# Seven block products for eight in the first matrix product of a two-pass feed-forward kernel

## The chip, the cores and the metric

One core of a Trainium2 chip runs the whole kernel. The metric is the device time of one execution in microseconds (us), given as the median of several runs. TensorE (PE) multiplies, with its weight loads shown apart (PEld); VectorE (DVE), ScalarE (ACT) and GpSimd (POOL) do the element-wise work; SyncE's queue (SP) issues every DMA.

## What is computed

A windowed attention (8 batches, 8 heads, 512 local and 32 global rows, head size 64) gives 8 x 544 rows of 512 numbers. A feed-forward layer follows, and it is most of the work:

```python
x = np.ascontiguousarray(attn_out.transpose(0, 2, 1, 3)).reshape(B * S, H * D)   # 4352 x 512
h = x @ w_in                                                                     # 512 -> 2048
sp = np.maximum(h, 0.0) + np.log1p(np.exp(-np.abs(h)))
g = h * erf(sp)
return (g @ w_out).astype(np.float32)                                            # 2048 -> 512
```

The weights arrive as 64-bit floats and are turned into 32-bit ones on the chip.

## The kernel before

**Products.** Every operand of the feed-forward layer is split into a high and a low part (`xh`/`xl`, `winh`/`winl`, `gh`/`gl`, `wouth`/`woutl`), and a product is three matmuls: high by high, high by low, low by high. One matmul is 128x128 weights by 512 columns.

**Two passes.** The 2048 hidden columns are halved; pass one takes the first 1024 for all chunks, pass two the rest. A chunk is one batch's 512 local rows (c = 0 to 7); chunk 8 holds the 256 global rows of all batches. Per chunk `load_x` (L633) fetches x^T from the scratch `xsc` and splits it; `unit` (L666) makes 128 hidden columns of h^T, four K-blocks by three matmuls, so 12 in one PSUM bank of the pool `ps_h` (2 banks), and copies the bank to `hs`; a chunk has 8 units, 96 matmuls. `gate` (L692) runs softplus and erf on four units in one ACT block (into `sp`), multiplies by h, and splits into `gh`/`gl`. `project` (L733) makes the second product in four banks of `ps_a` (6 banks): 4 row tiles by 4 pairs of units by 6 matmuls, again 96. Chunk 8 has 4 units of 24 matmuls on 256 columns, and 48 matmuls in `project`. In pass one `project` writes its sum to the scratch `part`; in pass two it loads that into `pr` and adds it (`os<-op,pr`) before the store.

**Stages.** Pass one also holds the attention of all batches, whose steps fill the engines between the units. When the attention is done (the mark `ATTN`), `load_late` (L802) converts the weights of pass two: `load_w` (L584) loads 64-bit numbers into `raw` (3 buffers), builds the 32-bit number in `top_...` with four DVE operations, and splits it. Five of the eight late units are converted in pass one, the rest at the start of pass two.

**Order.** `Program.schedule` (L129) writes out the order of each engine's instructions by a list schedule: every step has a key (its due time, some 5.4 us each), a planned duration for each engine that may run it, and inputs and outputs; at each planned moment an engine takes the ready step with the lowest key. A result that another engine hands to PE counts as ready 0.8 later (`SLACK`). The engines then run in that fixed order and wait for each other on semaphores. Chunk c of pass ps starts at key s = 4(17 ps + 2c); its units lie at s to s+7, its projection from s+8.29 on in steps of 2.

Of the kernel before, what the change touches and what calls it, by code (L numbers as in the profile page):

```python
# [20 lines left out]
P = 128  # L21
WB = 32
# [3 lines left out]

SINCE, COLD, FILL, TICK, HEAT = 0.75, 3.5, 50.0, 3.41, 3200
# [6 lines left out]
WB0, WBS = 50.7, 3.09  # L34
# [206 lines left out]
def kernel(  # L241
# [342 lines left out]
    def load_w(key, src, name, HI, LO, i, deps):  # L584
        RAW = mbuf([P, 512], I64, f"raw_{name}", "raw", 3)
        load(key - RLEAD, RAW, src, 524, deps, also=[HI, LO])
        TOP = mbuf([P, 512], I32, f"top_{name}", ("wt", "wr")[i % 2], 1)
# [4 lines left out]
        add({"ACT": 0.7}, key, lambda: act(HI.ap[:, i, :], word(1).bitcast(F32), AF.Abs), [RAW], [HI])  # L592

        def bits():
            dve.tensor_scalar(
                TOP.ap, word(1), 3, 0x3FFFFFF8, op0=ALU.logical_shift_left, op1=ALU.bitwise_and
            )
            dve.scalar_tensor_tensor(
                TOP.ap, word(1), s32(0xC0000000), TOP.ap, op0=ALU.bitwise_and, op1=ALU.bitwise_or
            )  # L600
            dve.scalar_tensor_tensor(
                TOP.ap, word(0), 29, TOP.ap, op0=ALU.logical_shift_right, op1=ALU.bitwise_or
            )

        def normal():
            a = TOP.ap.bitcast(F32)
            dve.scalar_tensor_tensor(
                a, HI.ap[:, i, :].bitcast(F32), NORMAL, a, op0=ALU.is_gt, op1=ALU.mult
            )

        add({"DVE": 1.55}, key, bits, [RAW], [TOP])
        add({"DVE": 0.6}, key, normal, [HI], [TOP])
        add({"ACT": 0.62, "DVE": 0.35}, key, lambda e: copy(e, HI.ap[:, i, :], TOP.ap.bitcast(F32)), [TOP], [HI])
        add(
            {"POOL": 1.27, "DVE": 0.6},
            key,
            lambda e: vec[e].tensor_tensor(
                LO.ap[:, i, :], TOP.ap.bitcast(F32), HI.ap[:, i, :].bitcast(F32), ALU.subtract
            ),
            [HI, TOP],  # L620
            [LO],
        )

# [9 lines left out]
    def load_x(ps, c, key):  # L633
# [3 lines left out]
        for i in range(2):  # L637
            RAW = mbuf([P, 2 * SL], F32, f"rx_{ps}_{c}_{i}", "raw", 3)
# [27 lines left out]
    def unit(ps, c, v, X, key):  # L666
# [21 lines left out]
        SPb = mbuf([P, SL], F32, f"sp_{nm}", "sp", 7)  # L688
        add({"ACT": 0.58, "DVE": 0.69}, key, lambda e: copy(e, Hb.ap, HP.ap.rearrange("p a t -> p (a t)")), [HP], [Hb])
        return Hb, SPb  # L690

    def gate(ps, c, us, key, first):  # L692
        def erf():
            table(SET_SOFTPLUS)
            for Hb, SPb in us:
                act(SPb.ap, Hb.ap, AF.Softplus)
            table(SET_ERF)
            for _, SPb in us:
                act(SPb.ap, SPb.ap, AF.Erf)
            if ps == 0:  # L700
                table(SET_EXP)
# [5 lines left out]
            [TAB, *(x[0] for x in us)],  # L707
            [x[1] for x in us],
        )
        G = []  # L710
        for v, (Hb, SPb) in enumerate(us, first):
            nm = f"{ps}_{c}_{v}"
            k = key + 0.01 * v
            GH = mbuf([P, SL], F32R, f"gh_{nm}", "gh", 5)
            GL = mbuf([P, SL], F32R, f"gl_{nm}", "gl", 5)
            add({"DVE": 0.75, "POOL": 1.5}, k, lambda e, SPb=SPb, Hb=Hb: vec[e].tensor_tensor(SPb.ap, SPb.ap, Hb.ap, ALU.mult), [Hb], [SPb])
            add({"DVE": 0.43, "ACT": 0.62}, k, lambda e, SPb=SPb, GH=GH: copy(e, GH.ap, SPb.ap), [SPb], [GH])
            add({"DVE": 0.75, "POOL": 1.5},
                k,
                lambda e, SPb=SPb, GH=GH, GL=GL: vec[e].tensor_tensor(GL.ap, SPb.ap, GH.ap.bitcast(F32), ALU.subtract),  # L720
# [3 lines left out]
            G.append((GH, GL))  # L724
# [8 lines left out]
    def project(ps, c, G, key):  # L733
# [3 lines left out]
        def mm2(t, u):  # L737
            WH, WL = W["out", ps, u]
            for a in range(2):
                GH, GL = G[2 * u + a] if c < B else G[u]  # L740
                s0 = P * t + (0 if c < B else 256 * a)
                lh, ll = (g.ap[:, s0 : s0 + P] for g in (GH, GL))
                first = u == 0 and a == 0
                last = u == NU - 1 and a == 1
                pe(OP[t].ap, lh, WH.ap[:, a, :], start=first, stop=False)
                pe(OP[t].ap, lh, WL.ap[:, a, :], start=False, stop=False)
                pe(OP[t].ap, ll, WH.ap[:, a, :], start=False, stop=last)

        for t in range(nt):
            if c == B:  # L750
                at = lambda u: key + u + 0.01 * t
            else:
                at = lambda u: key + 2 * u + 0.01 * t
            for u in range(NU):
                Gs = [x for g in (G[2 * u : 2 * u + 2] if c < B else G[u : u + 1]) for x in g]
                add({"PE": 1.37}, at(u), lambda t=t, u=u: mm2(t, u), [*Gs, *W["out", ps, u]], [OP[t]], heat=3072)
            k = at(NU - 1)
            O = mbuf([P, DM], F32, f"os_{ps}_{c}_{t}", "os", 2)
# [43 lines left out]
    def load_late(i):  # L802
        kind, src, u = ("in", w_in, i) if i < NU else ("out", w_out, i - NU)
        load_unit(kind, src, 1, u, late[2 * i], late[2 * i + 1], WB0 + WBS * i, [ATTN])

    late = [(wb_pool, f"b{i}") for i in range(11)] + [
        (wpool, t) for t in ("ih0", "il0", "ih1", "il1", "ih2")
    ]
    for i in range(2 * NU):
        if i < 5:  # L810
            load_late(i)
    for ps in range(2):
        for c in range(NCHT):
            s = NU * (17 * ps + 2 * c)
            n = NV if c < B else NU
            if ps == 1 and c == 0:
                for i in range(5, 2 * NU):
                    load_late(i)
            X = load_x(ps, c, s - XLEAD)
            us = [unit(ps, c, v, X, s + v) for v in range(n)]  # L820
            last = ps == 1 and c == NCHT - 1
            G = []
            for a, z in ((0, 2), (2, 3), (3, 4)) if last else [(i, i + 4) for i in range(0, n, 4)]:
                G += gate(ps, c, us[a:z], s + z + GOFF, a)
            project(ps, c, G, s + 4 + POFF)
# [76 lines left out]
```

## Time and profile before

| | us |
|---|---|
| median of 3 runs | 976.32 (976.29 to 978.1) |
| span of the profiled execution | 971.6 |
| PE busy | 937.7 (97%) |
| DVE, ACT, POOL busy | 553.7, 537.8, 308.3 |
| DMA | 127.6 MB, 41.9% of 16 engines |

```profile
PE   8977998999999999999999999999999999999996
DVE  5888999682665674855965399233424342333332
PEclk9988999999999999999999999999999999999998
DMA  9788956481475644823431233113314040311203
```

Each digit is one fortieth of the span (24.3 us) in tenths. Attention and pass one's projections fill the left half; pass two begins near 577 us, in the 24th digit.

### The profile page before, as it was taken

What the parts mean: (1) busy time and instruction counts of PE and PEld (TensorE: products, weight loads), DVE (VectorE), ACT (ScalarE), POOL (GpSimd) and SP (SyncE); (2) the same over time, 40 slices, a digit from 0 to 9 for tenths busy, and PEclk for the clock granted to TensorE, in tenths of its full rate; (3) what the DMA queues carried; (4) which work ended last, traced back from release to release, by engine and by line L of the source; (5) the groups of instructions that cost most, each with busy time, mean ns of one, the idle gap of its engine ahead of it and who ended that gap; (6) DMA issues with size and microseconds to landing.
All of it is one profiled execution on the core that took longest, in us unless ns stands there. A gap on an engine that the chain in (4) does not pass through costs nothing.

```text
span 971.6 us, 22208 instructions
## 1 busy us (share of the span) xinstructions
PE 937.7 (97%) x9068; PEld 757.9 (78%) x9068; DVE 553.7 (57%) x1386; ACT 537.8 (55%) x876; POOL 308.3 (32%) x230
## 2 busy tenths in 40 slices
PE   8977998999999999999999999999999999999996
PEld 6756766778777777778888888888888888888895
DVE  5888999682665674855965399233424342333332
ACT  4354685454646445736777656545655454555670
POOL 2242473322242232322533246312214221212140
PEclk9988999999999999999999999999999999999998
DMA  9788956481475644823431233113314040311203
GB/s 348 229 267 265 316 148 213 125 280 28 143 223 152 183 147 133 253 68 100 152 108 44 91 129 128 65 32 98 86 45 131 1 131 0 109 46 42 87 1 108
DMA packets 79741, 127.63 MB, mean 131 GB/s; under 512 B 12184, under 2 KB 37784, under 8 KB 79640
## 3 DMA queue, kind: packets, MB, share of 16 engines
q1 hardware_dynamic: 79640, 126.22, 41.9%
q8 instruction: 71, 1.16, 0.5%
q14 instruction: 30, 0.25, 0.1%
HBM read 99.45 MB, written 26.74 MB: 130 GB/s over the span
## 4 chain that ended last, share of the span: by engine, by line
PE 87%; DVE 6%; DMA 4%; issue 1%; ACT 1%; SPq 0%; DVEq 0%; ACTq 0%
PE op L279 38%; PE h L279 35%; PE o L279 3%; PE s L279 3%; PE t L280 2%; PE spare L279 2%; DVE top_out L291 2%; PE ga L279 1%; DMA rx<-xsc 1%; PE go L279 1%; DMA xsc<-xT 1%; PE gt L280 1%; DVE top_in L291 1%; DVE sm L291 1%; DMA part<-os 1%
## 5 line engine op out<-in xcount | busy, mean ns | idle before, releaser
L279 PE MATMUL h<-xh,winh 128*128 128x512 f32 (+1 forms) x576 | 221.1, 384 | 0.0
L279 PE MATMUL h<-xh,winl 128*128 128x512 f32 (+1 forms) x576 | 217.8, 378 | 0.0
L279 PE MATMUL h<-xl,winh 128*128 128x512 f32 (+1 forms) x576 | 217.6, 378 | 0.0
L279 PE MATMUL op<-wouth,gh 128*128 128x512 f32 x544 | 217.1, 399 | 0.2 <-DVE pt L291 0.2
L279 PE MATMUL op<-wouth,gl 128*128 128x512 f32 x544 | 212.2, 390 | 0.0
L279 PE MATMUL op<-woutl,gh 128*128 128x512 f32 x544 | 212.1, 390 | 0.0
L291 POOL TENSOR_TENSOR sp<-sp,hs 128x512 f32<-128x512 f32 x73 | 105.6, 1468 | 220.8 <-ACT sp L281 220.8
L291 DVE TENSOR_TENSOR gl<-sp,gh 128x512 fp32r<-128x512 f32 x77 | 70.4, 918 | 109.1 <-ACT gh L281 108.7
L281 ACT ACTIVATE gh<-sp 128x512 fp32r<-128x512 f32 x124 | 74.7, 627 | 98.9 <-PE op L279 76.6
L281 ACT ACTIVATE hs<-h 128x512 f32<-128x512 f32 x82 | 48.9, 597 | 137.6 <-PE h L279 137.4
L279 PEld LDWEIGHTS h<-xh,winh 128*128 128x128 f32 x576 | 108.4, 188 | 21.1 <-issue 0.8
L279 PEld LDWEIGHTS h<-xh,winl 128*128 128x128 f32 x576 | 108.4, 188 | 20.4
L279 PEld LDWEIGHTS h<-xl,winh 128*128 128x128 f32 x576 | 108.6, 188 | 19.4
L291 POOL TENSOR_TENSOR gl<-sp,gh 128x512 fp32r<-128x512 f32 x59 | 86.1, 1464 | 112.9 <-ACT gh L281 90.6
L279 PEld LDWEIGHTS op<-wouth,gh 128*128 128x128 f32 x544 | 102.2, 188 | 22.7 <-issue 1.0
L279 PEld LDWEIGHTS op<-wouth,gl 128*128 128x128 f32 x544 | 102.2, 188 | 21.9
L279 PEld LDWEIGHTS op<-woutl,gh 128*128 128x128 f32 x544 | 102.3, 188 | 19.3
L282 ACT ACT_TABLE_LOAD x90 | 115.5, 1283 | 2.3 <-PEq L889 0.7
L291 DVE COPY hs<-h 128x512 f32<-128x512 f32 x54 | 37.1, 686 | 110.8 <-PE h L279 110.6
L291 POOL TENSOR_TENSOR xl<-rx,xh 128x512 fp32r<-128x512 f32 (+1 forms) x40 | 52.3, 1328 | 119.4 <-ACT xh L281 72.8
L291 POOL TENSOR_TENSOR sm<-sm,mx 128x512 f32<-128x512 f32 x34 | 38.3, 1130 | 139.4 <-DVE mx L291 95.9
L291 DVE TENSOR_TENSOR sp<-sp,hs 128x512 f32<-128x512 f32 x63 | 61.0, 986 | 31.6 <-ACT sp L281 31.5
(75 smaller groups left out, 1212.4 us busy)
## 6 DMA issues: line engine op xcount, KB each, us to landing
vb<-in_vB_dram SPq DMA_DIRECT2D x64, 325.0 KB, 3.6
rx<-xsc SPq DMA_DIRECT2D x32, 512.0 KB, 4.8
va<-in_vA_dram SPq DMA_DIRECT2D x64, 195.0 KB, 3.9
k<-in_kE_dram SPq DMA_DIRECT2D x32, 384.0 KB, 5.6
q<-in_qT_dram SPq DMA_DIRECT2D x32, 272.0 KB, 4.6
part<-os SPq DMA_DIRECT2D x34, 256.0 KB, 3.0
pr<-part SPq DMA_DIRECT2D x34, 256.0 KB, 3.5
out_dram<-os SPq DMA_DIRECT2D x34, 256.0 KB, 3.7
```

Source lines behind the costliest of these rows:

```text
L279: pe = lambda n, *a, **k: pinned(nc.tensor.matmul(n, *a, **k))
L280: tr = lambda *a, **k: pinned(nc.tensor.transpose(*a, **k))
L281: act = lambda *a, **k: pinned(nc.scalar.activation(*a, **k))
L282: table = lambda name: pinned(nc.scalar.preload_act_table_set(name))
L291: return lambda *a, **k: pinned(f(*a, **k))
```

## The change

Pass two's local rows are taken by pairs of batches (chunks 2pr and 2pr+1). The pair's first product is a 2x2 by 2x2 block product: the weight blocks are hidden columns v and v+4 (rows of blocks) by the two halves of K, the other factor is the two halves of K by the two batches. Strassen's scheme in Winograd's form makes it with seven block products in place of eight. One **quad** q (of 4) stands for units q and q+4 of both batches: seven products of 6 matmuls, 42 where four units had 48.

- **Weights** (`convert_in`). Seven forms (three blocks as they are, four sums) are built after `ATTN` at keys 46.5 and 54.5, split, and written to the scratch `wq`, two tiles of 896 KB a quad. `quad_weights` loads both before each quad (two buffers each); the first two quads of pair 0 use the tiles as they were built. The four units of `w_out` are converted at keys 71 to 74.
- **The pair's other factor** (`pair_blocks`). Four 512 KB loads, four sums, seven blocks split into high and low. Each block has one buffer.
- **Products.** Banks a and c lie in `ps_h`, b and d in `ps_a`. Banks a, c and d are used twice: the first product is read out (`move` or `fold`), then a second is added on top in the same bank and read out again. Two moves (ACT or DVE) and five folds (DVE: bank plus an SBUF tile) replace four copies.
- **Keys.** Quad q of a pair lies at s+4q, s = 68+16pr; its gates at s+11, +17, +20, +25; its two projections from s+15 and s+23 on. `project` takes its units in the order 0, 2, 1, 3, loads the partial sum straight into `os` (4 buffers, before 2) and adds in place.
- **Global rows** of pass two stay last; they use four of the seven weight forms and the same number of matmuls. In pass one they come before the last batch.
- `raw` has 5 buffers in place of 3, and a scratch area for DMA descriptors is cut to 1024 bytes.

The diff, cut to its core:

```diff
+RAWS = 5
...
-WB0, WBS = 50.7, 3.09
+CV0, CVS, CVO = (46.5, 54.5), 1.8, (71.0, 72.0, 73.0, 74.0)
+QLEAD2, XDEL = 4.0, 1.6
+GATE1, GATE2, PROJ1, PROJ2 = (11.0, 17.0), (20.0, 25.0), 15.0, 23.0
+LAST = (0, 2, 1)
...
+class Part:
+    def __init__(self, whole, n):
+        self.whole, self.n, self.pool = whole, n, None
+        self.writers, self.readers = [], []
+    @property
+    def ap(self):
+        return self.whole.ap[:, self.n]
...
-        RAW = mbuf([P, 512], I64, f"raw_{name}", "raw", 3)
+        RAW = mbuf([P, 512], I64, f"raw_{name}", "raw", RAWS)
...
-    def project(ps, c, G, key):
+    def project(ps, c, G, at, order, after=None):
...
+            for n, rows in enumerate(order):
+                need = [x for g, _, v in rows for x in (*G[g], *W["out", ps, v // 2])]
+                add(
+                    {"PE": 0.685 * len(rows)},
+                    at(n) + 0.01 * t,
+                    lambda t=t, n=n: mm2(t, n),
+                    list(dict.fromkeys(need)) + ([PART[after, t]] if after is not None and n == 0 else []),
+                    [OP[t]],
+                    heat=1536 * len(rows),
+                )
+            k = at(len(order) - 1) + 0.01 * t
+            O = mbuf([P, DM], F32, f"os_{ps}_{c}_{t}", "os", 4)
...
-                PR = mbuf([P, DM], F32, f"pr_{c}_{t}", ("wt", "wr")[t % 2], 1)
-                load(k - NU + 2, PR, part[c][P * t : P * t + P, :], 262, [PART[c, t], W["out", 1, NU - 1][1]])
+                load(k - NU + 2, O, part[c][P * t : P * t + P, :], 262, [PART[c, t]])
...
-                    lambda t=t, O=O, PR=PR: dve.tensor_tensor(O.ap, OP[t].ap, PR.ap, ALU.add),
-                    [OP[t], PR],
-                    [O],
+                    lambda t=t, O=O: dve.tensor_tensor(O.ap, OP[t].ap, O.ap, ALU.add),
+                    [OP[t]],
+                    [O, PART[c, t]],
...
+    NQ = NU
+    A11, A12, A22, S1, S2, S3, S4 = range(7)
+    wq = [[dram.tile([P, 7, 2, P], F32, name=f"wq{q}_{x}") for x in range(2)] for q in range(NQ)]
+    WQ = {(q, x): fixed(None) for q in range(NQ) for x in range(2)}
...
+    def convert_in(u, key):
+        top = lambda n: View(Buf(wb_pool, [P, 512], F32, f"c{n}_{u}", f"x{n}", 1))
+        T = {}
+        for n, (v, i) in enumerate(((u, 0), (u + 2, 0), (u + 2, 1), (u, 1))):
+            T[v - u, i] = top(n)
+            ABS = View(Buf(wb_pool, [P, 512], F32, f"ca_{u}_{n}", "x5", 1))
+            to_fp32(key + CVS * n, w_in[1, v, i], f"l_in_{v}_{i}", T[v - u, i], ABS, [ATTN])
...
+        a11, a12, a21, a22 = T[0, 0], T[0, 1], T[2, 0], T[2, 1]
+        part_of(A11, a11, key)
+        k = key + 2 * CVS
+        part_of(A22, a22, k)
+        sum_of(s1, a21, a22, ALU.add, k)
+        sum_of(a21, a11, a21, ALU.subtract, k)
+        part_of(S1, s1, k + 0.3)
+        part_of(S3, a21, k + 0.6)
+        sum_of(a11, s1, a11, ALU.subtract, k + 0.9)
+        part_of(S2, a11, k + 1.2)
+        k = key + 3 * CVS
+        part_of(A12, a12, k)
+        sum_of(a12, a12, a11, ALU.subtract, k + 0.3)
+        part_of(S4, a12, k + 0.6)
...
+                    lambda x=x, t=t, q=2 * u + r: dma(wq[q][x], t.ap.bitcast(F32)),
+                    [t],
+                    [WQ[2 * u + r, x]],
+                    moved=918.0,
...
+    def quad_weights(name, q, key):
+        HL = [Buf(wb_pool, [P, 7, 2, P], F32R, f"wq{x}_{name}", f"q{x}", 2) for x in range(2)]
+        for x, t in enumerate(HL):
+            add(
+                {"SP": 0.06},
+                key,
+                lambda x=x, t=t: dma(t.ap.bitcast(F32), wq[q][x]),
+                [WQ[q, x]],
+                [t],
+                moved=918.0,
+            )
+        return HL
...
+        k = key + 0.2
+        block("B11", 0, R[0, 0], k)
+        sum_of(T, R[0, 1], R[0, 0], ALU.subtract, k)
+        sum_of(R[0, 1], R[1, 1], R[0, 1], ALU.subtract, k + 0.1)
+        block("T1", 3, T, k + 0.1)
+        sum_of(T, R[1, 1], T, ALU.subtract, k + 0.1)
+        block("T2", 1, T, k + 0.1)
+        block("B21", 2, R[1, 0], k + 0.2)
+        block("B22", 4, R[1, 1], k + 0.3)
+        block("T3", 5, R[0, 1], k + 0.4)
+        sum_of(R[1, 0], R[1, 0], T, ALU.subtract, k + 0.4)
+        block("T4", 6, R[1, 0], k + 0.5)
+        return blocks
...
+    def products(name, q, X, key, held=None):
+        QH, QL = held or quad_weights(name, q, key - QLEAD2)
+        bank = {
+            n: Buf(pool, [P, SL], F32, f"p{n}_{name}", tag, m)
+            for n, (pool, tag, m) in zip("abcd", ((ps_h, "h", 2), (ps_a, "a", 6)) * 2)
+        }
+        def mm(n, m, x, start):
+            o, (HI, LO) = bank[n].ap, X[x]
+            for j in range(2):
+                wh, wl = (t.ap[:, m, j, :] for t in (QH, QL))
+                xh, xl = HI.ap[:, j, :], LO.ap[:, j, :]
+                more = dict(skip_group_check=True)
+                pe(o, wh, xh, start=start and j == 0, stop=False, **more)
+                pe(o, wh, xl, start=False, stop=False, **more)
+                pe(o, wl, xh, start=False, stop=j == 1, **more)
+        def product(n, m, x, start, k):
+            add({"PE": 1.37}, k, lambda: mm(n, m, x, start), [QH, QL, *X[x]], [bank[n]], heat=3072)
...
+        PAIR = mbuf([P, 2, SL], F32R, f"pair_{name}", ("xh", "xl")[q % 2], 3)
+        V, Z = Part(PAIR, 0), Part(PAIR, 1)
+        f32 = lambda b: b.ap.bitcast(F32) if b in (V, Z) else b.ap
...
+        k = [key + 4 * i / 7 for i in range(7)]
+        product("a", A11, "B11", True, k[0])
+        move(U, "a", k[0])
+        product("b", S2, "T2", True, k[1])
+        fold(U, U, "b", k[1])
+        product("a", A12, "B21", False, k[2])
+        move(C, "a", k[2])
+        product("c", S1, "T1", True, k[3])
+        fold(V, U, "c", k[3], [PAIR])
+        product("d", S3, "T3", True, k[4])
+        fold(V, V, "d", k[4])
+        product("c", S4, "B22", False, k[5])
+        fold(Z, U, "c", k[5])
+        product("d", A22, "T4", False, k[6])
+        fold(U, U, "d", k[6])
+        return (C, U), (Z, V), PAIR
...
+            for i, (m, x) in enumerate((((A11, "B1"), (A12, "B2")), ((S1, "B1"), (A22, "D")))[r]):
...
+    s = -NV
+    for c in [*range(B - 1), B, B - 1]:
+        s += NU if c == B - 1 else NV
+        n = NV if c < B else NU
+        X = load_x(0, c, s - XLEAD)
+        us = [unit(0, c, v, X, s + v) for v in range(n)]
+        G = {}
+        for a in range(0, n, 4):
+            G |= gate(0, c, us[a : a + 4], s + a + 4 + GOFF)
+        key = s + 4 + POFF
+        if c < B:
+            project(0, c, G, lambda n: key + 2 * n, [[(2 * u + a, 0, 2 * u + a) for a in range(2)] for u in range(NU)])
+        else:
+            project(0, c, G, lambda n: key + n, [[(u, 256 * a, 2 * u + a) for a in range(2)] for u in range(NU)])
+    for u in range(2):
+        first = convert_in(1 - u, CV0[u])
+    for n, u in enumerate((0, 2, 1, 3)):
+        load_unit("out", w_out, 1, u, (wpool, f"oh{u}"), (wpool, f"ol{u}"), CVO[n], [ATTN])
+    s0 = 17 * NU
+    turns, ACTS = (), fixed(None)
+    AFTER = {0: first[0], 1: [W["out", 1, u][1] for u in LAST]}
+    for pr in range(B // 2):
+        s = s0 + 4 * NU * pr
+        X = pair_blocks(pr, s - XDEL)
+        one, two = [], []
+        for q in range(NQ):
+            a, b, more = products(f"{pr}_{q}", q, X, s + 4 * q, first.get(q) if pr == 0 else None)
+            one += [(q, a[0], ()), (q + 4, a[1], ())]
+            two += [(q, b[0], (more,)), (q + 4, b[1], (more,))]
+        order = [[(v, 0, v) for v in (2 * u, 2 * u + 1)] for u in (0, 2, 1, 3)]
+        for us, c, g, at in ((one, 2 * pr, GATE1, PROJ1), (two, 2 * pr + 1, GATE2, PROJ2)):
+            G = {}
+            for h in range(2):
+                turn = fixed(None)
+                G |= gate(1, c, us[4 * h : 4 * h + 4], s + g[h], turns, [turn], [ACTS])
+                turns = [turn]
+            project(1, c, G, lambda n: s + at + 2 * n, order, c - 1 if c else None)
+    s = s0 + 4 * NU * (B // 2)
+    X = last_blocks(s - XLEAD)
+    us = [last_unit(q, X, s + q) for q in range(NQ)]
+    G = {}
+    for a, z in ((0, 2), (2, 3), (3, 4)):
+        G |= gate(1, B, us[a:z], s + z + GOFF)
+    key = s + 4 + POFF
+    project(1, B, G, lambda n: key + n, [[(q, 0, q), (q, 256, q + 4)] for q in range(NQ)])
...
-    nc = _bacc.Bacc("TRN2", target_bir_lowering=False, num_devices=1)
+    nc = _bacc.Bacc("TRN2", target_bir_lowering=False, num_devices=1, dynamic_dma_scratch_size=1024)
```

## Rows read from the trace of the kernel before

**Rows 1.** The page: span and busy time of each engine.
```profile
span 971.6 us, 22208 instructions
PE 937.7 (97%) x9068; PEld 757.9 (78%) x9068; DVE 553.7 (57%) x1386; ACT 537.8 (55%) x876; POOL 308.3 (32%) x230
```
**Rows 2.** Windows: from:to, length, busy (instructions), granted clock, DMA share, GB/s; seven of pass two, summed.
```profile
600.00:650.00 50.00, 50.00 (x222) 41.44 (x221) 18.39 (x24) 25.39 (x40) 17.19 (x12) 1.00 0.16 53
...
sum 350.00, PE 350.00 PEld 291.86 DVE 126.05 ACT 185.24 POOL 95.49; mean PE 50.00 PEld 41.69 DVE 18.01 ACT 26.46 POOL 13.64
```
**Rows 3.** Windows of pass one's start, and of the end.
```profile
0.00:50.00 50.00, 43.88 (x959) 34.70 (x959) 34.31 (x134) 19.81 (x38) 12.55 (x15) 0.97 0.84 282
50.00:100.00 50.00, 40.76 (x818) 30.61 (x815) 41.97 (x163) 25.56 (x58) 17.54 (x16) 0.86 0.88 278
...
950.00:971.60 21.60, 12.41 (x55) 9.95 (x53) 3.41 (x5) 0.63 (x1) 0.00 (x0) 0.88 0.35 117
```
**Rows 4.** Chain that ended last, around pass two's first `h`: start, us, what.
```profile
512.17 5.44 PE h L279 x24
517.62 5.44 PE op L279 x24
...
576.82 8.16 PE h L279 x36
```
**Rows 5.** Windows around the start of pass two.
```profile
560.00:580.00 20.00, 20.00 (x107) 17.28 (x106) 19.19 (x25) 11.72 (x17) 7.95 (x5) 1.00 0.34 105
580.00:600.00 20.00, 20.00 (x90) 16.54 (x89) 19.69 (x20) 15.64 (x26) 14.75 (x10) 1.00 0.39 134
```
**Rows 6.** Tiles of pass two, 600 to 950 us: durations in ns, min/median/max.
```profile
L291 DVE TENSOR_TENSOR os<-op,pr x30: 676/691/693, 650.3 to 948.9; 128x512 f32<-128x512 f32 x30
L281 ACT ACTIVATE hs<-h x39: 575/598/604, 606.1 to 942.0; 128x512 f32<-128x512 f32 x39
L291 DVE TENSOR_TENSOR gl<-sp,gh x45: 678/693/1595, 605.7 to 938.6; 128x512 fp32r<-128x512 f32 x45
L291 DVE CAST xh<-rx x14: 285/418/1003, 609.5 to 876.1; 128x512 fp32r<-128x512 f32 x12, 128x256 fp32r<-128x256 f32 x2
L291 DVE TENSOR_TENSOR xl<-rx,xh x16: 414/677/1236, 610.2 to 919.8; 128x512 fp32r<-128x512 f32 x14, 128x256 fp32r<-128x256 f32 x2
L291 POOL TENSOR_TENSOR xl<-rx,xh x14: 1191/1294/1303, 612.0 to 877.5; 128x512 fp32r<-128x512 f32 x12, 128x256 fp32r<-128x256 f32 x2
```
**Rows 7.** DVE timeline, one conversion of half a late unit: start, us.
```profile
569.37 0.43 DVE L291 TENSOR_SCALAR top_out<-raw_out 128x512 int32<-128x512 int32 x1
569.83 1.42 DVE L291 SCALAR_TENSOR_TENSOR top_out<-raw_out,top_out 128x512 int32<-128x512 int32 x2
571.35 0.69 DVE L291 SCALAR_TENSOR_TENSOR top_out<-wouth,top_out 128x512 f32<-128x512 f32 x1
```
**Rows 8.** DMA issues of 600 to 950 us: KB each, median us to landing.
```profile
pr<-part SPq DMA_DIRECT2D x32, 256.0 KB, 3.5
out_dram<-os SPq DMA_DIRECT2D x29, 256.0 KB, 3.8
rx<-xsc SPq DMA_DIRECT2D x11, 512.0 KB, 4.8
```
**Rows 9.** Timeline of the end: start, us, what.
```profile
962.02 0.39 PE L279 MATMUL op<-wouth,gl 128*128 128x512 f32 x1
962.45 0.69 DVE L291 TENSOR_TENSOR os<-op,pr 128x512 f32<-128x512 f32 x1 [0.67 <-PE op L279]
```
**Rows 10.** Chain that ended last, a hand-over from ACT to PE.
```profile
65.33 0.94 ACT xn L281 x4
66.27 0.04 issue
66.32 1.12 PE t L280 x4
```
**Rows 11.** Waits of PE over the span, the longest: us, times, longest.
```profile
PE t L280 <- ACT xn L281: 3.5, 2, 2.6
```

More of the change, by code (lines that the diff above doesn't have):

```diff
@@ L582, in mbuf, with to_fp32 @@
         return Buf(mp, shape, dtype, name, tag, bufs)
[L584 to L587 removed]
+    def to_fp32(key, src, name, TOP, ABS, deps):
+        RAW = mbuf([P, 512], I64, f"raw_{name}", "raw", RAWS)
+        load(key - RLEAD, RAW, src, 524, deps, also=[TOP.buf, ABS.buf])
         def word(n):
@@ L605, in normal @@
-        def normal():
[L606 to L613, printed above, removed]
+            top = TOP.ap().bitcast(I32)
+            dve.tensor_scalar(top, word(1), 3, 0x3FFFFFF8, op0=ALU.logical_shift_left, op1=ALU.bitwise_and)
@@ new lines, in bits @@
+            dve.scalar_tensor_tensor(
+                top, word(1), s32(0xC0000000), top, op0=ALU.bitwise_and, op1=ALU.bitwise_or
+            )
+            dve.scalar_tensor_tensor(top, word(0), 29, top, op0=ALU.logical_shift_right, op1=ALU.bitwise_or)
+        def normal():
+            a = TOP.ap()
+            dve.scalar_tensor_tensor(a, ABS.ap().bitcast(F32), NORMAL, a, op0=ALU.is_gt, op1=ALU.mult)
+        add({"DVE": 1.55}, key, bits, [RAW], [TOP.buf])
+        add({"DVE": 0.6}, key, normal, [ABS.buf], [TOP.buf])
@@ L614, in load_w, with split @@
+    def split(key, TOP, HI, LO):
+        add({"ACT": 0.62, "DVE": 0.35}, key, lambda e: copy(e, HI.ap(), TOP.ap()), [TOP.buf], [HI.buf])
         add(
@@ L723, in gate @@
             )
-            G.append((GH, GL))
+            G[v] = (GH, GL)
         return G
@@ new lines, in mm2 @@
+        def mm2(t, n):
+            for m, (g, c0, v) in enumerate(order[n]):
+                WH, WL = W["out", ps, v // 2]
+                s0 = P * t + c0
+                lh, ll = (x.ap[:, s0 : s0 + P] for x in G[g])
+                first = n == 0 and m == 0
+                last = n == len(order) - 1 and m == len(order[n]) - 1
+                pe(OP[t].ap, lh, WH.ap[:, v % 2, :], start=first, stop=False)
+                pe(OP[t].ap, lh, WL.ap[:, v % 2, :], start=False, stop=False)
+                pe(OP[t].ap, ll, WH.ap[:, v % 2, :], start=False, stop=last)
@@ L801 @@
     add({"SP": 0.01}, HKEYS[-1][1] + 0.5, lambda: None, [], [ATTN])
[L802 to L825, printed above, removed]
+    NQ = NU
@@ new lines, in last_blocks, with block @@
+    def last_blocks(key):
+        n = B * SG
+        blocks, R = {}, []
+        for i in range(2):
+            R.append(mbuf([P, 2, n], F32, f"rg_{i}", "raw", RAWS))
+            R[i].view = None
+            load(key + 0.1 * i, R[i], xsg[2 * P * i : 2 * P * i + 2 * P, :].rearrange("(k p) t -> p k t", p=P), 525, XSG)
+        def block(name, m, A, k):
+            HI, LO = (Buf(pool, [P, 2, n], F32R, f"g{x}_{name}", tag) for x, (pool, tag) in zip("hl", XTAG[2 * m : 2 * m + 2]))
+            add({"DVE": 0.5, "ACT": 0.62}, k, lambda e: copy(e, HI.ap, A.ap), [A], [HI])
+            add(
+                {"POOL": 1.3, "DVE": 0.7},
+                k,
+                lambda e: vec[e].tensor_tensor(LO.ap, A.ap, HI.ap.bitcast(F32), ALU.subtract),
+                [A, HI],
+                [LO],
+            )
+            blocks[name] = (HI, LO)
+        block("B1", 0, R[0], key + 0.2)
+        block("B2", 1, R[1], key + 0.3)
+        add({"DVE": 0.7}, key + 0.3, lambda: dve.tensor_tensor(R[1].ap, R[1].ap, R[0].ap, ALU.subtract), [R[0]], [R[1]])
+        block("D", 2, R[1], key + 0.4)
+        return blocks
```

183 lines of the change are left out of this document (134 added, 49 removed).

## The prediction

> **What bounds the kernel now.** I read the page's busy times first: PE works 937.7 of 971.6 us, no other engine more than 57% [rows 1]. [...] The chain that ended last says the same: it runs from one run of matmuls to the next, 24 of them in 5.44 us, in `h` and in `op` alike [rows 4]. That is 0.2267 us a matmul. The waits of PE, the longest of them 3.5 us in all [rows 11], are all in attention steps. [...]
>
> **What is removed.** A pair of batches has 2 x 96 = 192 first-product matmuls before and 4 quads x 7 products x 6 = 168 after. Four pairs save 4 x 24 = 96 matmuls of the full 512 columns, 96 x 0.2267 = **21.8 us** [rows 4]. The second product and the global rows keep their count. In pass two PE has no idle time to hide this in, so it all lies on the path [rows 2]. [...]
>
> **Element-wise work in the loop.** Per pair: 16 copies of h go (0.60 us on ACT, 0.69 on DVE) [rows 6]; 8 moves come (4.8 us) and 20 folds. A fold reads one bank and one SBUF tile as `os<-op,pr` does, 0.69 us, so 13.8 us on DVE. Blocks are 14 half-tiles instead of 8: six more casts (0.42 to 0.60 each) and six more low parts (0.68 on DVE, 1.29 on POOL), 7 to 11 us. Four sums of 1024 columns are twice the 0.68 or 1.29 each, 5 to 10 us. Against 10 us removed that is some +25 us a pair, over three engines. Before, a pair's time (2 x 192 x 0.2267 = 87 us) holds (126 + 185 + 95)/350 x 87 = 101 us of such work [rows 2]; after, about 126 in three times 81.6 us. DVE goes from 36% to some 58%. No engine becomes the bound of the loop, so this costs nothing as throughput, and the cover is PE's own work. What it can cost is latency, next.
>
> **The reused banks.** In a quad three products (the third, sixth and seventh) go into a bank that must be read first: 16 quads x 3 = 48 new waits of PE on ACT or DVE. The same wait, `h` on a read of its bank, exists before, but with a second bank free. Between the first use and the reuse lies at least one other product, 6 x 0.2267 = 1.36 us. Needed are the hand-over from PE (the last matmul starts at 962.02 and lasts 0.39, the DVE step starts at 962.45, so 0.04) [rows 9], the read, 0.69 [rows 6], and the hand-over back, 0.05 by the step from ACT to PE [rows 10]: 0.78 us, which leaves 0.58. A longer operation may sit ahead in DVE's queue: `gl<-sp,gh` has a median of 0.69 but a maximum of 1.60 us [rows 6]. With one such ahead the wait is up to 1.0 us; with a group of the second product (1.36 us) also between, there is none. The planner counts a result for PE as ready 0.8 late, so it places such a group whenever one is ready, and from the second quarter of a pair on one nearly always is (keys s+7 to s+13 and s+15 to s+21 overlap the quads). Bounds for the loop: 0 and 48 x 1.0 = 48 us. I take **+1.5**, near the lower end, since the nearest wait of that kind, on `h` banks, is zero in 350 us [rows 2].
>
> **The streamed weights.** 18 quad loads of 1.8 MB, 33 MB in 386 us (576.8 to 962.4 [rows 4, 9]), add some 86 GB/s to the 53 of the first window of pass two [rows 2]. That is well under the 282 GB/s that the first 50 us moved [rows 3]. One quad's two tiles take between 1.8 MB / 282 GB/s = 6.5 us and, by 512 KB in 4.8 us [rows 8], twice 8.4 us; I take 8. A load may start when the quad two before it is done; the quad between lasts 9.5 us alone and some 20 with its share of projections. In the loop that is hidden. SP issues in order, so behind a load that waits for its buffers stand the partial sums and the stores; the partial sums (3.5 us) are asked for two keys, some 10 us, ahead [rows 8]. Nothing in the loop.
>
> **The start of pass two.** This is where I put the largest loss. DVE is busy 19.2 and 19.7 of 20 us there already [rows 5], and PE is not held up, because its queue is deep. After the change the conversions of `w_in` come earlier, where there is room, but all four units of `w_out` are converted here: 8 halves at 0.43 + 1.42 + 0.69 = 2.5 us on DVE [rows 7], 20 us, and casts and low parts besides. Add pair 0's blocks (14 casts, 14 low parts, 4 sums: 21 to 37 us over the three engines), 14 us of folds and the last batch's gate. In the meantime PE has pass one's last projection (96 matmuls, 21.8 us) and the four quads (38.1 us), and no projection of pass two before key 83, so for some two quads there is no filler: 6 waits of 0 to 1.0 us, and a wait of quad 3 for its weights of 0 to 7 us (16.8 against 9.5). Between 0 and 13 us; I take **+3**, since the same saturation costs nothing before.
>
> **Pass one and the end.** Two more `raw` buffers let two 512 KB weight loads, 1.0 MB or 3.7 us at 282 GB/s, go out ahead of attention's loads where DMA is the limit [rows 3]. That can delay attention by up to 3.7 us, or bring later weights and x in earlier by as much: -4 to +4, I take **+1**. The global chunk moved ahead of the last batch brings the same matmuls; nothing. At the end the same four-tile projection, now of batch 7, ends last instead of two tiles: the chain after the last matmul, DVE 0.69 and a store of 3.8 us [rows 8, 9], stays. Six partial sums share four `os` buffers there, so one may load only after a store: 0 to 3 us, I take **+0.5**.
>
> **Sum.** -21.8 + 1.5 + 3 + 1 + 0.5 = -15.8 us. The span goes from 971.6 to 955.8. The median lies 4.7 us above the profiled span (976.3 - 971.6), so 960.5.
>
> **The rivals.**
> - *The start of pass two runs dry.* DVE's backlog there (for it: 39 of 40 us busy [rows 5]; against it: no wait of PE in the same stretch) costs its full 13 us and the waits of the loop a few more: 6 us more than I took to 15 more, 967 to 976.
> - *All hidden, and pass one gains.* No new wait, and the earlier weight loads bring the -4: 976.3 - 21.8 - 4 = 950.5. For it: PE waits for nothing after attention [rows 2]. Against it: the first stage is full of DMA, and bytes do not shrink [rows 3].
> - *Slower: the reused bank.* At its place, the third, sixth and seventh product of a quad, PE stands until DVE has worked off two operations. Two at 1.0 us over the cover of 0.58, plus the fold, is a wait of about 1.0 us; at 48 places 48 us, at half of them 24, which gives 976.3 - 15.8 + 24 = 984.5. It decides from 21.8/48 = 0.45 us a wait, less 0.1 for the other losses. Against it: the room of 1.36 us that each filler gives, and DVE at 58%. [...]
> - *No change.* The order written out places the quads' work so that the saved matmuls reappear as idle time of the same length, at any mixture of the places above: 976 within 2.
>
> **How the numbers follow.** My forecast, 952.5 to 967, gets 0.58; the dry start 0.17, of which 0.02 within the band of no change; all hidden 0.10; slower 0.12, of which 0.02 within the band; no change 0.03. The range 950.5 to 974 holds the forecast, 0.14 of the dry start and 0.08 of the all-hidden case, together 0.80. A difference of 0.2% (2 us) is about what a measurement of this kernel can tell from none. Faster by more: 0.58 + 0.10 + 0.15 = 0.83. Within: 0.02 + 0.02 + 0.03 = 0.07. Slower: 0.10.
>
> **What would show it.** In the profile of the changed kernel pass two should have 672 product matmuls of 512 columns besides the global rows, 0.227 us apart, with windows of PE at 50.00 of 50 between the second pair and the last. Waits of PE on DVE or ACT steps that write `u`, `c` or `pair` are the reused banks: under 2 us in all if I am right, over 20 if the slower case holds. Waits on `wq` DMAs would be the streamed weights. The first 60 us of pass two should hold what loss there is, and DVE should be near full in them. Pass one's end (the last `h` of its units) within 4 us of before confirms that term. I would be wrong most likely through DVE's plan: its steps are planned at 0.72 or 0.75 us, and where POOL runs beside it they last up to 1.6 [rows 6].

## The result and the profile after

The changed kernel takes **966.35 us** (median of 4 runs, 964.19 to 969.97) against 976.88 us: ratio **0.9902**, 95% interval 0.9874 to 0.9929. That is 10.5 us less, where 15.8 were forecast; it lies within the range. A second set of runs beside the experiments gave 0.9909 (0.9878 to 0.9940). The profiled execution spans 962.2 us, 9.4 less than before [rows 1].

The page's busy times, and three of its rows of 40 slices:

```profile
span 962.2 us, 22283 instructions
PE 920.8 (96%) x8962; PEld 740.6 (77%) x8962; DVE 645.2 (67%) x1488; ACT 536.1 (56%) x886; POOL 394.1 (41%) x289
...
PE   8988989989999999999999999979999999999996
...
DVE  5799888954476575754777799799556446544462
...
PEclk9999999999999999999999999998999999999998
```

PE is busy 16.9 us less, not 21.8, and idle 41.4 us instead of 33.9 [rows 1]. The 7 in PE's row is the 27th slice, 626 to 650 us: the start of pass two, with DVE at 7 to 9 tenths around it. The windows say where (from:to, length, busy of PE, PEld, DVE, ACT, POOL with instructions, granted clock, DMA share, GB/s):

```profile
620.00:630.00 10.00, 6.12 (x26) 4.76 (x25) 8.82 (x11) 4.35 (x9) 6.41 (x5) 0.98 1.01 398
630.00:640.00 10.00, 10.00 (x39) 8.06 (x38) 8.91 (x14) 3.31 (x7) 2.26 (x2) 0.85 0.43 149
640.00:650.00 10.00, 7.30 (x33) 5.71 (x31) 10.00 (x8) 7.49 (x12) 8.77 (x6) 1.00 0.45 177
650.00:660.00 10.00, 8.88 (x27) 7.07 (x28) 10.00 (x9) 4.04 (x8) 9.36 (x7) 0.66 0.00 0
...
560.00:720.00 160.00, 151.32 (x644) 123.23 (x643) 125.92 (x150) 83.60 (x132) 82.71 (x52) 0.97 0.49 178
720.00:900.00 180.00, 180.00 (x810) 149.63 (x809) 94.70 (x124) 96.71 (x148) 86.06 (x60) 1.00 0.46 162
```

From 720 to 900 us, where the last two pairs of batches run, PE is busy 180.00 of 180 at a granted clock of 1.00, as in [rows 2]. Between 560 and 720 it lacks 8.7 us of busy time. With each of the two long stands the granted clock falls (0.85 and 0.66 in the windows of 10 us): the next 8 and 13 matmuls run at 0.50 (the windows of these matmuls stand in the last section). Waits of PE over 560 to 720 us (us in total, times, longest), and the one kind after it:

```profile
PE pc L295 <- DVE pair L307: 4.0, 2, 3.9
PE pa L295 <- DVE u L307: 3.8, 1, 3.8
PE pd L295 <- DVE pair L307: 0.8, 1, 0.8
...
PE h_g L295 <- DMA wq_g<-wq: 1.7, 2, 1.5
```

The first three are the reused banks: a product that must wait for a fold or a move. They add up to 8.6 us, where the prediction named under 2 us as the sign that it was right and over 20 as that of the slower rival. The timeline shows what DVE did instead (start, us, what; its idle time before in brackets):

```profile
617.66 1.57 DVE L307 TENSOR_SCALAR top_out<-raw_out 128x512 int32<-128x512 int32 x1
619.26 1.42 DVE L307 SCALAR_TENSOR_TENSOR top_out<-raw_out,top_out 128x512 int32<-128x512 int32 x2
620.60 0.42 DVE L307 TENSOR_SCALAR top_out<-raw_out 128x512 int32<-128x512 int32 x1
621.05 2.48 DVE L307 SCALAR_TENSOR_TENSOR top_out<-raw_out,top_out 128x512 int32<-128x512 int32 x2
...
628.31 0.69 DVE L307 TENSOR_TENSOR pair<-u,pc 128x512 f32<-128x512 f32 x1
629.05 0.50 PE L295 MATMUL pc<-xh_B,wq 128*128 128x512 f32 x1 [3.88 <-DVE pair L307]
...
641.85 5.82 DVE L307 CAST xh_B<-rx 128x512 fp32r<-128x512 f32 x4
647.59 2.88 DVE L307 CAST xh_T<-rt 128x512 fp32r<-128x512 f32 x2
650.39 0.68 DVE L307 COPY u<-pa 128x512 f32<-128x512 f32 x1
651.12 0.79 PE L295 MATMUL pa<-xh_B,wq 128*128 128x512 f32 x1 [3.83 <-DVE u L307]
```

Two things stand ahead of the fold in DVE's queue: conversions of `w_out`, and then the next pair's casts, six in 8.6 us (641.85 to 650.47), 1.44 us each on average while POOL works beside them, where the median before is 0.42 [rows 6].

**An account by stage.** I counted in the traces how many matmuls of the two products are still to start at a given moment, each start once and a 256-column one as half. A stretch of length L in which the number falls by N has lost L - N x 0.2267 us (0.2267 us a matmul, as in [rows 4]). A 256-column matmul takes 0.12 us, a little over the half, so the global rows show some 0.6 us that nobody lost.

| | left at 450 | left at 560 | left at 720 | lost 560 to 720 | left at 900 | last starts |
|---|---|---|---|---|---|---|
| before | 2253 | 1770 | 1065 | 0.2 | 271 | 962.0 |
| changed | 2141 | 1659 | 1017 | **14.5** | 224.5 | 953.5 |

With 96 matmuls less, 1674 would be left at 560; the 15 below that are 3.4 us gained in pass one. Then 14.3 us are lost to the start of pass two, 0.3 from 720 to 900, and 2.1 from there to the end of the last matmul (3.0 against 1.0; 1.7 of it are the waits on `wq_g`, at a granted clock of 1.00 from 900 to 950 us), while what follows the last matmul is 0.9 shorter. -21.8 - 3.4 + 14.3 + 0.3 + 2.1 - 0.9 = -9.4, the difference of the spans.

### The profile page after: what moved, and what is told of

Its sections match the earlier page's. It is cut to its first block, busy times and chain, and to the rows that moved or that the text cites. A ratio compares the mean times of both kernels' runs of the same rounds, so it can differ in the third digit from the quotient of the medians.

```text
span 962.2 us, 22283 instructions
## 1 busy us (share of the span) xinstructions
PE 920.8 (96%) x8962; PEld 740.6 (77%) x8962; DVE 645.2 (67%) x1488; ACT 536.1 (56%) x886; POOL 394.1 (41%) x289
## 4 chain that ended last, share of the span: by engine, by line
PE 81%; DVE 10%; DMA 5%; issue 2%; ACT 1%; SPq 1%; POOL 0%; DVEq 0%; ACTq 0%; POOLq 0%
PE op L295 35%; PE h L295 16%; PE pd L295 4%; PE pc L295 4%; PE pa L295 4%; PE o L295 3%; PE s L295 3%; PE t L296 2%; DVE top_out L307 2%; PE pb L295 2%; PE spare L295 2%; PE ga L295 1%; DMA raw_out<-in_w_out_dram 1%; DMA vb<-in_vB_dram 1%; DVE xl_T L307 1%
## 5 line engine op out<-in xcount | busy, mean ns | idle before, releaser
L295 PE MATMUL h<-xh,winh 128*128 128x512 f32 (+1 forms) x288 | 112.3, 390 | 0.0
L295 PE MATMUL h<-xh,winl 128*128 128x512 f32 (+1 forms) x288 | 109.0, 378 | 0.0
L295 PE MATMUL h<-xl,winh 128*128 128x512 f32 (+1 forms) x288 | 108.9, 378 | 0.0
L307 POOL TENSOR_TENSOR sp<-sp,hs 128x512 f32<-128x512 f32 x40 | 59.8, 1515 | 51.5 <-ACT sp L297 51.5
L297 ACT ACTIVATE sp<-sp 128x512 f32<-128x512 f32 x136 | 74.9, 620 | 0.4
L307 DVE CUSTOM_DVE_ANT_0 sm<-s,cs 128x128 f32<-128x128 f32 x256 | 57.8, 284 | 21.7 <-PE s L295 18.4
L297 ACT ACTIVATE sm<-sm 128x512 f32<-128x512 f32 x64 | 39.9, 630 | 44.0 <-POOL sm L307 31.6
L295 PEld LDWEIGHTS h<-xh,winl 128*128 128x128 f32 x288 | 54.2, 188 | 10.5
L295 PEld LDWEIGHTS h<-xh,winh 128*128 128x128 f32 x288 | 54.3, 188 | 10.3 <-issue 0.8
L295 PEld LDWEIGHTS h<-xl,winh 128*128 128x128 f32 x288 | 54.3, 189 | 9.1
```

What stands on the lines that cost most here:

```text
L295: pe = lambda n, *a, **k: pinned(nc.tensor.matmul(n, *a, **k))
L297: act = lambda *a, **k: pinned(nc.scalar.activation(*a, **k))
L307: return lambda *a, **k: pinned(f(*a, **k))
```

## The experiments

Three theories for these 14 us, which the expectations below call 13. **DVE queue**: at the start of pass two DVE has too much work, and the folds stand behind it. **Stream**: weights or x arrive late. **Bank**: returning to a bank costs by itself. The last has the trace against it already (nothing lost in 180 us of the loop). Ratios are to runs of the kernel before on the same chip; the changed kernel's are 0.9902 and 0.9909. The counts come from one profiled execution of each run. It is the fastest of four of the changed kernel, the slowest of four in e1, v0 and v1, the fastest of ten in e3 and in e5 order, so counts and ratios need not add up.

| run | ratio (95%) | left at 450, 560, 720 | lost 560 to 720 |
|---|---|---|---|
| changed, again | 0.9909 (0.9878 to 0.9940) | 2142, 1660, 1018 | 14.5 |
| e1 less conversion | 0.9790 (0.9736 to 0.9845) | 2154, 1672, 1004 | 8.6 |
| e2 casts on ACT | 0.9844 (0.9805 to 0.9883) | 2146, 1664, 996 | 8.6 |
| e3 keys spread | 0.9935 (0.9910 to 0.9960) | 2121, 1639, 1016 | 18.8 |
| e4 both | 0.9906 (0.9877 to 0.9935) | 2128, 1646, 1001 | 13.8 |
| e5 raw 3 | 1.0102 (1.0071 to 1.0133) | 2129, 1647, 1091 | 34.0 |
| e5 order | 1.0036 (1.0009 to 1.0064) | 2123, 1640.5, 1061 | 28.6 |
| e6 double stream | 0.9997 (0.9966 to 1.0027) | 2139, 1657, 1025 | 16.7 |
| v0 early | 0.9770 (0.9747 to 0.9793) | 2137, 1655, 957 | 1.8 |
| v2 early, 4 forms | 0.9749 (0.9720 to 0.9778) | 2148, 1666, 968 | 1.8 |
| v1 early, 4 forms, ACT | 0.9773 (0.9730 to 0.9815) | 2160, 1678, 982 | 2.2 |
| v3 as v2, old order | **0.9704** (0.9661 to 0.9747) | 2140, 1657, 952 | 0.2 |

**The changed kernel again.**

> The changed kernel as it is, once more beside the others, for a comparison on the same chip. All theories: 0.990 of before, within 0.003, with some 13 us lost between 560 and 720 us.

It gave 965.35 us and the same stands.

**Less conversion work, same order of instructions.**

```diff
         def bits():
...
             dve.tensor_scalar(top, word(1), 3, 0x3FFFFFF8, op0=ALU.logical_shift_left, op1=ALU.bitwise_and)
+            if name.startswith("out_1"):
+                return
...
         def normal():
+            if name.startswith("out_1"):
+                return
```

> Same order of instructions as the changed kernel, but the late conversion of w_out does only the first of its four DVE operations (the number's other bits are left out, so the output is not the reference's); 8 x (1.42 + 0.69) = 17 us of DVE work leave the start of pass two. Theory 'DVE queue': the folds come earlier, the stand of 3.9 us behind top_out goes with its slow-clock tail, the one behind the casts shrinks; 5 to 9 us below the changed kernel's 966.4, so 957 to 961. Rival 'stream' (weights and x arrive late in the full DMA of 620 to 630 us): 966 within 2. Rival 'bank' (the return to the same bank costs by itself): 966 within 2.

956.24 us, a little better than the best expected. The waits of PE between 560 and 720 us:

```profile
PE pa L295 <- DVE u L307: 3.3, 1, 3.3
PE pc L295 <- DVE pair L307: 1.6, 2, 1.4
```

The stand behind `top_out` fell from 4.0 to 1.6 us and the other stayed, 3.3. Every DMA and every matmul stands where it stood in the order, so neither stream nor bank can explain it. 5.9 us of the 14.5 came back. The profiled execution (960.08) spans 4.1 us less than the changed kernel's: its pass one is 13 matmuls, 2.9 us, behind, and 0.8 more are lost from 720 to 900; 1.5 less after that and 0.4 less behind the last matmul make up the sum. Where the further gain of the median lies is not shown.

**Casts on ACT.**

```diff
-            add({"DVE": 1.2, "ACT": 1.22}, k, hi, [A], [HI])
+            add({"ACT": 1.22}, k, lambda: hi("ACT"), [A], [HI])
```

> The high parts of the pair blocks are cast on ACT only (planned 1.22), so the DVE casts that last 1.44 us a half beside POOL go. Theory 'DVE queue': the stand of 3.8 us behind xh_B and xh_T goes, the other stays: 3 to 6 us below the changed kernel, 960 to 963. Rival 'stream': 966 within 2. Rival 'bank': 966 within 2.

961.11 us. The stand behind the casts is gone, and the one behind the conversions, which was expected to stay, with it; others took part of their place:

```profile
PE pc L295 <- DVE xl_T L307: 2.1, 2, 1.6
PE pa L295 <- ACT c L297: 0.7, 1, 0.7
PE pc L295 <- ACT xh_T L297: 0.7, 1, 0.7
```

Now the first products of pair 1 wait for their blocks, and the loop loses 3.5 us from 720 to 900. Because the planned durations changed, so did the whole order; this run shows less than the one before it.

**Conversions spread over more keys, alone and (the second run) with the casts on ACT.**

```diff
-CV0, CVS, CVO = (46.5, 54.5), 1.8, (71.0, 72.0, 73.0, 74.0)
+CV0, CVS, CVO = (46.5, 54.5), 1.8, (71.0, 74.5, 78.0, 81.5)
```

> The four conversions of w_out get the keys 71, 74.5, 78 and 81.5 instead of 71 to 74. Theory 'DVE queue': less in front of the folds of quads 1 to 3, 3 to 7 us below the changed kernel, 959 to 963. Rival 'stream': the raw loads are spread as well, so 0 to 4 below. Rival 'bank': 966 within 2.

> Casts on ACT and the conversions spread, together. Theory 'DVE queue': most of the 13 us lost at the start of pass two comes back: 8 to 12 below, 954 to 958. Rival 'stream': at most 4 below. Rival 'bank': 966 within 2.

Both missed: 968.9 and 964.47 us. The first stand is gone, and 15.1 of the 18.8 us of the keys-spread run are lost between 640 and 680 us instead:

```profile
PE pc L295 <- ACT xh_T L297: 4.2, 1, 4.2
PE pd L295 <- POOL xl_T L307: 2.3, 2, 1.7
PE pb L295 <- DVE os L307: 1.7, 1, 1.7
...
640.00:680.00 40.00, 30.69 (x110) 22.63 (x111) 37.85 (x35) 21.52 (x34) 29.18 (x18) 0.83 0.16 51
```

The longest are waits for pair 1's blocks. The code holds their loads back until three units of `w_out` are converted (`AFTER`), but that is not the reason: the four loads start no later than in the changed kernel (first line that kernel's, second line this run's).

```profile
619.55 4.41 SPq L299 DMA_DIRECT2D rx<-xsc  x4
616.62 4.12 SPq L299 DMA_DIRECT2D rx<-xsc  x4
```

What is later is the last conversion, whose low part ends at 645.3 us instead of 635.9, and the casts and low parts of the blocks stand beside and behind it, with DVE busy 37.85 of 40 us. So my expectation was too narrow: it is not only the folds that are queued behind the conversions. Moving the work within the start moves the wait; the amount of it has to go.

**Stage by stage undone: three raw buffers, and the old order of pass one.**

```diff
-RAWS = 5
+RAWS = 3
...
-            R[i, j] = mbuf([P, 2, SL], F32, f"rx_1_{c}_{i}", "raw", RAWS)
+            R[i, j] = mbuf([P, 2, SL], F32, f"rx_1_{c}_{i}", *(("rawb", 2) if n == 3 else ("raw", RAWS)))
...
-        T = mbuf([P, 2, SL], F32, f"rt_{pr}", "raw", RAWS)
+        T = mbuf([P, 2, SL], F32, f"rt_{pr}", "rawb", 2)
```

> The changed kernel with three raw buffers for the weights and x, as before the change, and two of their own for the pair's last load and sums. Theory 'raw buffers': the 2 to 3 us that pass one gained (about 11 matmuls ahead at 450 us) come from earlier loads, so the lead is gone and the time is 2 to 3 us above the changed kernel's 0.990 of before, 0.992 to 0.993. Rival 'order of the list schedule': the lead comes from steps that fell differently, nothing systematic, 0.990 within 0.003 and the lead in matmuls anywhere between -15 and +25.

982.93 us, ratio 1.0102: 2% above the changed kernel, which neither case forecast. The lead of pass one did not vanish, it grew: 2129 left at 450 us where the changed kernel has 2141. The raw buffers are not its cause. At 450 us the runs lie between 2121 and 2160, 39 matmuls or 8.8 us apart, and runs that share pass one's order (changed, again, e1, e6: 2139 to 2154) already 3.4 us. The lead of 3.4 us in pass one is no larger than that. What the five shared buffers do buy (the edit keeps five, but splits them into three and two) is at the start of pass two, where 34.0 us are lost without them: there the pair's loads, the sums and the conversions of `w_out` share them. Pair 1's loads start at 637 to 647 us here instead of 620 to 624, and the first product of one quad waits 3.2 us for its two weight tiles, the only waits of a quad on `wq` in any run.

```diff
-    for c in [*range(B - 1), B, B - 1]:
-        s += NU if c == B - 1 else NV
+    for c in range(NCHT):
+        s += NV
```

> The changed kernel with the global rows of pass one last again, as before the change. Theory 'DVE queue': the last batch's gate then lies 4 keys earlier and the start of pass two is less crowded, since the global chunk has half the element-wise work: 1 to 4 us below the changed kernel, 0.986 to 0.989 of before. Rival 'filler': the small projection of the global rows gives PE only 48 matmuls beside the first quads instead of 96, and the start runs dry earlier, 2 to 6 us above.

977.61 us, the rival's side and far beyond it: by the ratios 13 us above the changed kernel. I had costed this move at nothing. Waits of PE from 560 to 720 us, and the longest in the timeline:

```profile
PE pa L295 <- DVE u L307: 5.7, 1, 5.7
...
PE pd L295 <- POOL xl_T L307: 3.8, 2, 3.3
PE pa L295 <- DVE xh_B L307: 3.6, 1, 3.6
PE op L295 <- ACT gh L297: 3.3, 1, 3.3
...
667.55 0.80 PE L295 MATMUL pa<-xh_B,wq 128*128 128x512 f32 x1 [5.73 <-DVE u L307]
```

At this place the second product of a bank follows the first with no other matmul between; in the changed kernel at least 6 lie between everywhere.

**The stream doubled.**

```diff
-                lambda x=x, t=t: dma(t.ap.bitcast(F32), wq[q][x]),
+                lambda x=x, t=t, d=dram.tile([P, 7, 2, P], F32, name=f"dup_{name}_{x}"): (
+                    dma(t.ap.bitcast(F32), wq[q][x]), dma(d, wq[q][x])),
```

> Every load of quad weights is issued together with a copy of the same 896 KB from scratch to scratch, so the streamed bytes double (33 MB more read, 33 MB more written). Theory 'DVE queue': outside the global rows, whose weights are late already (1.7 us), nothing waits for these loads; 0 to 5 us above the changed kernel, all of it in waits on wq of the global rows and at the end. Rival 'stream' (loads late in pass two): 10 us or more above, with waits of pa to pd on wq DMAs.

972.48 us, 6 to 7 above the changed kernel, and 9 by the ratios: more than expected, and close to the 10 of the rival, but not where the rival puts it. In the loop nothing is lost (720 to 900: 0.2 us), with DMA at 68%; at the start 2.2 us more than in the second set of the changed kernel. The rest lies after 900 us, 9.8 lost instead of 3.0 to 5.6:

```profile
PE h_g L295 <- DMA wq_g<-wq: 6.0, 3, 3.7
```

No product of the quads waits on a `wq` load, here or in the changed kernel, so the stream is not the cause of the 14 us; it is the cause of the small loss at the global rows.

**The conversion of w_out moved into pass one.** Each half is converted beside the attention, in the `gh` and `gl` buffers, written to scratch as high and low parts, and loaded ready at the old keys.

```diff
+    def convert_out(u, i, key):
...
+        H, L = (View(mbuf([P, 512], F32R, f"c{x}_{name}", f"g{x}", 5)) for x in "hl")
+        to_fp32(key, w_out[1, u, i], name, TOP, H, ())
+        split(key, TOP, H, L)
...
+                lambda x=x, t=t: dma(wo[u][x][:, i, :], t.ap().bitcast(F32)),
+    for n in range(2 * NU):
+        convert_out(n // 2, n % 2, 24.0 + 2.4 * n)
```

> The second half of w_out is converted in pass one (keys 24 to 40.8, beside the attention), written to scratch as high and low parts, and only loaded at the start of pass two; 8 conversions of some 3.5 us leave the start. Theory 'DVE queue': the stand behind top_out goes, 5 to 6 us below the changed kernel as in the run with the shortened conversion, 0.984 of before, if the attention pays nothing for the 20 us of DVE work; up to 5 us more if it does. Rival 'stream': the same bytes are loaded at the same keys, 0.990 within 0.003.

**950.97 us**, more than twice the gain expected. 1.8 us are lost between 560 and 720; the whole stretch in one window, and its waits of PE:

```profile
560.00:720.00 160.00, 158.85 (x700) 130.90 (x699) 95.54 (x116) 81.74 (x126) 81.60 (x52) 1.00 0.52 188
...
PE op L295 <- POOL gl L307: 0.6, 1, 0.6
PE op L295 <- ACT gh L297: 0.5, 1, 0.5
```

DVE has 96 us of work there instead of 126, at almost the same DMA traffic (188 against 178 GB/s). No reused bank waits any more, though the products and their banks are the same and lie as close (6 matmuls between at the closest, in both). That settles it between the three. What this run does not separate is two ways in which the conversions held DVE up: their own time, and the raw buffers and the hold (`AFTER`) by which pair 1's loads came late. Those loads start at 593.8 us here, not 619.5, its casts run from 623.0 to 639.8 us, not from 630.5 to 657.2, and only four of the fourteen fall to DVE instead of six; the order of all steps was planned anew. The run with less conversion work shows the first way alone (its loads start at 621.3 us, no earlier), worth 5.9 us. And the attention pays nothing: 2137 matmuls are left at 450 us, where the changed kernel has 2141.

**Four weight forms for the global rows; the casts on ACT besides; the old order besides.**

```diff
-    def quad_weights(name, q, key):
+    def quad_weights(name, q, key, n=7):
...
-                lambda x=x, t=t: dma(t.ap.bitcast(F32), wq[q][x]),
+                lambda x=x, t=t: dma(t.ap[:, :n].bitcast(F32), wq[q][x][:, :n]),
...
-        QH, QL = quad_weights(f"g{q}", q, key - QLEAD2)
+        QH, QL = quad_weights(f"g{q}", q, key - QLEAD2, 4)
```

> The early conversion of w_out as in the run before, and the global rows load only the four weight forms that they use (512 KB a tile instead of 896). Theory: the waits on wq_g (2.4 us) and the slow clock behind them, together 4 us between 720 and 900 us, go: 0.973 of before, 2 to 4 us below the run with the early conversion alone. Rival (the loads are late because they start late, not because of their size): 0.977, no change.

> As the run with four forms, and the casts of the pair blocks on ACT only. Theory 'DVE queue': with the conversions gone there is nothing left to win at the start (1.4 us lost there), so within 2 us of the run with four forms. Rival 'lock' (the casts lengthened beside POOL cost wherever they lie): 3 us below it.

> The run with early conversion and four weight forms, but with the global rows of pass one last again. In the changed kernel that order cost 13 us. Theory 'DVE queue': it cost that only because the folds stood behind conversions and PE had little else; with the conversions gone from the start the order is worth 0 to 3 us, 0.975 to 0.978 of before. Rival 'filler' (the quads need the 96 matmuls of the last batch's projection beside them, whatever DVE does): 8 us or more above the run with four forms, 0.983 or more.

The four forms gave 950.92 us against 950.97, where 2 to 4 less were expected: the waits on `wq_g` went from 2.4 us to none, and the 5.0 us that the run before lost from 720 to 900 to 0.7, but the intervals overlap, so a gain in time is not shown. The casts on ACT added nothing (953.42 us, 0.9773, interval across the other); there the loop itself loses 3.7 us, 2.0 of them waits of `pb` on `xl_T`. The old order, which cost 13 us before, now costs nothing: **947.44 us**, 0.9704, the fastest median of all and better than expected, though its interval still touches that of the run with four forms, with no wait of PE from 540 to 950 us:

```profile
560.00:720.00 160.00, 160.00 (x719) 132.94 (x718) 100.76 (x114) 84.38 (x131) 83.91 (x53) 1.00 0.51 188
```

So the last batch's projection was needed as filler only while the folds were late. This version beats the kernel before by 29 us, and the changed one by some 19.

## Why the prediction was right, and where it was off

- **The bound and the saving: right.** 720 to 900 us run at the rate of before [rows 2, 4], 0.2267 us a matmul with 0.3 us lost, with 42 matmuls a quad; the trace has the 672 product matmuls that were forecast, 96 fewer in all, and the whole saving shows in the last version, whose start loses nothing.
- **The reused banks: right in the loop, with its reason.** +1.5 forecast, 0.3 measured at most, because more lies between than the one product that I counted on: after 720 us at least 12 matmuls, 2.7 us, at every reuse. The mechanism of the slower rival is real all the same: it decided at the start, where all four of its waits in the changed kernel are.
- **The start of pass two: the step that was mis-sized.** I took +3 with bounds 0 to 13; it cost 14.3. I listed the work rightly (conversions, blocks, folds, and their sum), and then chose the lower end "since the same saturation costs nothing before". That reason does not carry: before, no product had to go back to the bank that it had just left. That PE's other waits for DVE had more room then is my reading; I did not measure it. Also, I bounded a wait by one long operation ahead (1.0 us). DVE's queue held a chain of them: at the two stands of 3.9 and 3.8 us, 12 and 30 matmuls (2.7 and 6.8 us) lay between the two uses of the bank, so the read was done only 6.7 and 10.7 us after the first use. And each of the two long stands has a spell at a granted clock of 0.50 (3.4 and 5.7 us) that I had not priced: the stretch lost 14.5 us and PE stood for 8.7 of them, and most of the other 5.8 is that, some 4.3 by the estimate of the last section. The last sentence of the prediction named the place: DVE's steps beside POOL, planned too short; in the profile of before a `gl` of DVE that starts at 938.57 us, beside a step of POOL, took 1.59 us, and here casts took 1.44.
- **The move of the global rows: costed at nothing, and wrong.** It brings the same matmuls, but it puts 96 of them beside the first quads where the old order has 48; undone, it costs 13 us. It was the cover that I should have named.
- **The stream: right for the quads, incomplete.** I compared the load (8 us) with a quad (9.5 us) but not with the global rows' units, which last 24 x 0.12 = 2.9 us: 1.7 us of waits, 2.1 in all (3.1 and 4.6 in the second set).
- **Pass one and the end.** +1 forecast, -3.4 measured, no more than runs of one order differ by; my mechanism, the raw buffers, fell. The sign that I named, the last `h` of pass one within 4 us of before, failed (563.4 against 571.1 us), but with the global rows moved it compares different work. The end came as its mechanism said and larger than its bound: the last partial sum finds its `os` buffer only when a store has landed. The chain that ended last:

```profile
949.25 6.27 DMA out_dram<-os
955.54 2.95 DMA os<-part
...
958.62 0.69 DVE os L307
```

PE is done at 953.9 us, so the last add comes 4.6 us late, not 0.5. What hid it in the account is the last store: it landed 2.9 us after its add here, and 8.5 us after it in the profile of before [rows 9]; why that one took so long is open. That the end came out 0.9 shorter is luck. A fifth and sixth `os` buffer were not tried.
- **The offset.** In the changed kernel's runs the time lies 1.9 to 2.1 us above the span. The 4.7 that I took from before was therefore for more than half a profiled execution faster than the median; the changed kernel's profile (964.19) is faster than its median too, by 2.2. This is why the medians differ by 10.5 and the spans by 9.4.

The forecast of 960.5 missed by 6 us, on the side of the rival "the start runs dry" (967 to 976), which is the case that came true in mechanism. That the time still lies within the range is partly luck: the start cost 11.3 us more than I took and the global rows 2.1, and 7.0 came back from pass one (4.4), the end (1.4) and the loop (1.2), the first two not by what I had foreseen.

## What to carry to other kernels

When a change makes the busiest engine wait for another in a tight loop, price that wait by the longest chain of work that the other engine's queue can hold at the worst place, not by its mean load, and look first where a phase begins. If such a place is overloaded, take work out of it, here a conversion that another phase had room for; spreading it inside the place only moves the wait. A step that "moves nothing but order" is worth what it puts beside the critical work.

## What the runs showed of the hardware

After each of the two stands of PE, of 3.9 and 3.8 us, the granted clock was 0.50 for 3.4 and 5.7 us:

```profile
629.60:633.00 3.40, 3.40 (x9) 2.64 (x8) 2.86 (x5) 2.05 (x4) 1.02 (x1) 0.50 1.05 387
651.10:656.80 5.70, 5.68 (x13) 4.46 (x14) 5.70 (x4) 1.31 (x3) 5.70 (x4) 0.50 0.00 0
```

Most matmuls in them start 0.43 us apart instead of 0.2267, so the two stands cost some 4.3 us more than they lasted: an estimate, (3.4 + 5.7) x (1 - 0.2267/0.43). Between 560 and 950 us DVE casts of 512 columns lasted 0.41 to 0.43 us with POOL idle, and 1.42 to 1.55 us (once 2.6) where POOL was busy all the time, while a fold, which reads one SBUF tile and a bank, never lasted longer than 0.69 us, beside POOL or not (ns, min/median/max):

```profile
L307 DVE TENSOR_TENSOR pair<-u,pc x32: 675/687/689, 584.9 to 885.6; 128x512 f32<-128x512 f32 x32
```

The last three of the six casts from 641.85 us on start 1.40 to 1.44 us after the one before them, as do POOL's instructions beside them; no run shows why. Loads of 896 KB landed after 6.3 us (median); a quad's two tiles, issued together, were both there after 6.7 to 7.8 us, close to the 8 taken. The 33 MB of them in pass two cost the loop nothing that shows: 0.3 us lost from 720 to 900 us, and 0.2 when doubled.
